# GpSimd drains, separate value banks and a split slot end in a chunked attention and mixture-of-experts kernel

## Chip, cores and metric

The kernel runs on one core of a Trainium2 chip. The metric is the device time of one execution in microseconds. The core's engines are TensorE (PE, matrix products; its weight loads are shown apart as PEld), VectorE (DVE), ScalarE (ACT), GpSimd (POOL) and SyncE (SP). Each engine works through an instruction queue of its own, and engines wait for each other and for transfers on semaphores. Sums of matrix products lie in PSUM banks of 128 x 512 floats.

## Reference

Attention within chunks of 64 positions, then a top-1 mixture of experts over the 4608 rows that come out. q, k and v are 8 x 8 x 576 x 64, the gate is 512 x 8, w1 is 8 x 512 x 1024 and w2 is 8 x 1024 x 512, all float32.

```python
# attention, chunk = 64
scores = scale * np.matmul(q_c, k_c.transpose(0, 1, 2, 4, 3))
scores = scores - np.max(scores, axis=-1, keepdims=True)
attn = np.exp(scores)
attn = attn / (np.sum(attn, axis=-1, keepdims=True) + 1e-09)
out = np.matmul(attn, v_c)
# mixture of experts on x = out as [4608, 512]
logits = x @ w_gate
expert_idx = np.argmax(logits, axis=1)
gate_w = softmax(logits)[row, expert_idx]
for e in range(E):
    h = np.maximum(x[mask] @ w1[e], 0.0)
    out[mask] = gate_w[mask, None] * (h @ w2[e])
```

## The kernel before

**Attention.** A loop of 18 steps (`for g in range(NG)`) takes 256 rows each. A step computes scores into bank pair psS, a softmax on DVE and ACT, transposes, and then `attn_v`: 32 small products of weights and values into the two-bank tile psX (`pair["X"]`), one bank for each half of the heads. `x_out` (L292 to L301) scales each bank on DVE by the softmax sums. Routing follows two steps behind, and GpSimd stores the rows sorted by expert into a scratch tensor `xd` with indirect transfers (L426).

**Experts.** The rows are then worked through in slots of 256 sorted rows. Slot 0 is filled into the end of the attention. The others are `slot(u, ...)` (L1061), of which 17 are executed here. A slot whose expert has a small rest takes 64 or 128 more rows (`form_x`), all others take `form_a`; which one is decided at run time by a branch. For each of 8 parts f of the hidden layer, `gemm1` makes 12 products into bank psS or psL. ACT takes the rectified value `hh`, DVE the remainder `hl`, and two parts later `gemm2` adds 3 products for each half m of the rows into banks U and V, which are the two halves of psX. All operands are split into a high and a low part, so each product is three.

**The end of a slot.** After the branch come, in the order in which they are written (the order on PE, DVE, ACT and POOL is that of the code): `make_xt(u + 1)` transposes the rows of the next slot on PE, ACT and DVE split them; `split_step(u, 7)` splits one weight chunk (ACT L74, DVE L75) and issues an indirect weight load on GpSimd (L530); blocks 6 and 7 of `gemm2`; then `finish` for m = 0 and 1: DVE scales the sums by the gate into y (L670), and GpSimd writes y to its rows of the output with an indirect transfer (L671).

**GpSimd's queue in a slot** holds, from there on: the weight load, two output transfers, three gathers of rows (L545, the third after the branch), three weight loads (L530), and, where a `form_a` branch has to count up a semaphore for the transfer that only `form_x` makes, an instruction that the profile calls INC_SWDGE_SEM (L1128). All 205 indirect transfers of an execution are issued by GpSimd. At the end of the program (L1153 for the slots that are not executed, L1185 for the end itself) GpSimd waits for its transfers, executes such an INC_SWDGE_SEM and a DRAIN, and then all engines meet.

Of the kernel before, what the change touches and what calls it, by code (L numbers as in the profile page):

```python
# [8 lines left out]
F32 = mybir.dt.float32  # L9
# [3 lines left out]
AF = mybir.ActivationFunctionType  # L13
ALU = mybir.AluOpType
# [4 lines left out]
P = 128  # L19
# [5 lines left out]
G = 2  # L25
# [20 lines left out]
def attn_moe_kernel(ctx: ExitStack, tc: tile.TileContext, q, k, v, wg, w, out):  # L46
    nc = tc.nc
# [29 lines left out]
    def split_half(c, m, buf):  # L77
# [6 lines left out]


    psa = ctx.enter_context(tc.tile_pool(name="psa", bufs=1, space=PSUM))
    pair = {"X": psa.tile([P, 2, 512], F32, name="psX")}
    one = {x: psa.tile([P, 512], F32, name=f"ps{x}") for x in "TQLK"}
    c2 = ExitStack()
    pss = c2.enter_context(tc.tile_pool(name="pss", bufs=1, space=PSUM))  # L90
    pair["S"] = pss.tile([P, 2, 512], F32, name="psS")

    slots = {"U": [pair["X"][:, 0, :]], "V": [pair["X"][:, 1, :]], "X": [one["L"]],
             "TQ": [one["T"], one["Q"]], **{x: [one[x]] for x in "TQLK"}}
    turns = {x: 0 for x in slots}
    psum = []

    def bank(tag, shape):
        n = 1
        for x in shape[1:]:  # L100
            n *= x
        if tag == "S":
            t = psum[0].tile([P, 512], F32, name="psS", tag="S", bufs=2)
        else:
            t = slots[tag][turns[tag] % len(slots[tag])]
            turns[tag] += 1
        t = t[0:shape[0], 0:n]
        if len(shape) == 3:
            t = t.rearrange("p (a b) -> p a b", b=shape[2])
        return t  # L110
# [5 lines left out]
    gate = [const.tile([P, 3], F32, name=f"gate{i}") for i in range(3)]  # L116
    oid = [const.tile([P, 3], I32, name=f"oid{i}") for i in range(3)]

    NK, NB = 3, 3
# [9 lines left out]
    vb = [kv.tile([P, G, 512], F32, name=f"vb{i}") for i in range(NB)]  # L129
# [83 lines left out]
    def quads(i, hp):  # L213
        for c in range(2):
            for m in range(2):
                o = hp * 128 + c * 64
                yield (slice(c * 64, (c + 1) * 64), m, slice((i * 4 + hp) * 64, (i * 4 + hp + 1) * 64),
                       slice(m * 64, (m + 1) * 64), slice(o, o + 64), (m * 64, c * 64))
# [5 lines left out]
                             ones.unsqueeze(1).broadcast_to([P, 4, P]), start=True, stop=True)  # L224

    def scores(g):
        ps = pair["S"]
        for i in range(G):
            for hp in range(4):
                for po, m, fo, pi, fi, at_ in quads(i, hp):  # L230
                    nc.tensor.matmul(ps[po, m, fo], qt[g][pi, i, fi], kb[g % NK][pi, i, fi],
                                     start=True, stop=True, tile_position=at_)
        return ps
# [37 lines left out]
    def attn_t(ex):  # L271
        at = sp.tile([P, G, 4, 128], F32, name="at", bufs=1)
        for i in range(G):
            pt = bank("TQ", [P, 4, 128])
            for hp in range(4):
                nc.tensor.transpose(pt[:, hp, :], ex[:, i * 4 + hp, :, :].rearrange("p m k -> p (m k)"), ident)
            nc.scalar.copy(at[:, i, :, :], pt)
        return at

    def attn_v(g, at):  # L280
        px = pair["X"]
        for i in range(G):
            for hp in range(4):
                for po, m, fo, pi, fi, at_ in quads(i, hp):
                    nc.tensor.matmul(px[po, m, fo], at[pi, i, hp, po], vb[g % NB][pi, i, fi],
                                     start=True, stop=True, tile_position=at_)
        return px

# [2 lines left out]
    def x_out(g, px, ri, xt):  # L291
        r0 = g * G % RB  # L292

        t = g * G - XB * RB
        assert t < 0 or t in stored
        for m in range(2):
            nc.vector.tensor_tensor(
                xt[:, r0:r0 + G, m * 256:(m + 1) * 256].rearrange("p i (h d) -> p i h d", d=64),
                px[:, m, :].rearrange("p (i h d) -> p i h d", i=G, d=64),
                ri[:, m * NH // 2:(m + 1) * NH // 2, :].rearrange("p (i h) o -> p i h o", i=G)  # L300
                .broadcast_to([P, G, 4, 64]), ALU.mult)  # L301

# [222 lines left out]
    def wset(u):  # L525

        return 0 if u < 2 else (u + 1) % 2
# [22 lines left out]
    def gather(u):  # L550
        for h in range(2):
            rows_in(xg[u % 2][h], u, h)
# [4 lines left out]
    def ids(u, t, h):  # L557

        nc.vector.tensor_copy(gate[u % 3][:, h:h + 1], t[:, D:D + 1])
        nc.vector.scalar_tensor_tensor(oid[u % 3][:, h:h + 1], past(u, h), BIG, t[:, D + 1:D + 2],  # L560
                                       ALU.mult, ALU.max)

    def make_xt(u, part=None, banks="TQ"):
        par = u % 2
        for h in range(2) if part is None else (part,):
            pg = bank(banks[h], [P, 4, 128])
            for kc in range(4):
                nc.tensor.transpose(pg[:, kc, :], xg[par][h][:, kc * 128:(kc + 1) * 128], ident)
            o = xhi[:, :, h * 128:(h + 1) * 128]
            nc.scalar.copy(o, pg)  # L570
            nc.vector.tensor_tensor(xlo[:, :, h * 128:(h + 1) * 128], pg, o.bitcast(F32), ALU.subtract)  # L571
            ids(u, xg[par][h], h)
# [92 lines left out]
        nc.tensor.matmul(py, hh, wl, start=False, stop=False)  # L665
        nc.tensor.matmul(py, hl, wh, start=False, stop=f == 7)  # L666

    def finish(u, m, py, n=P):
        y = yp.tile([P, D], F32, name=f"y{m}")[0:n, :]
        nc.vector.tensor_scalar(y, py, gate[u % 3][0:n, m:m + 1], None, ALU.mult)  # L670
        nc.gpsimd.indirect_dma_start(  # L671
            out=outs[m], out_offset=bass.IndirectOffsetOnAxis(ap=oid[u % 3][0:n, m:m + 1], axis=0),
            in_=y, in_offset=None,
            bounds_check=NT - 1, oob_is_err=False)
# [258 lines left out]
    for g in range(NG):  # L933
        ga, gl = g - 1, g - 2
        pace[0] = 1000
        ps = scores(g)
# [6 lines left out]
        if ga >= 0:  # L943
            at = attn_t(st_e[ga])
# [17 lines left out]
        if ga >= 0:  # L962
            px = attn_v(ga, at)
# [14 lines left out]
    g = NG - 1  # L978
# [5 lines left out]
    at = attn_t(ex)  # L984
# [11 lines left out]
    px = attn_v(g, at)  # L996
# [64 lines left out]
    def slot(u, kd, nxt):  # L1061
        par = wset(u)
        py = [bank("UV"[m], [P, D]) for m in range(2)]
        if u > 1:
            gather(u + 2)

        last = [[hq.tile([P, BLK], F32R, name=f"{x}{f}") for x in ("hh", "hl")] for f in (6, 7)]

        def block(f, h, ms=(0, 1)):
            for m in ms:  # L1070
                gemm2(par, f, h, m, py)

        def later():

            if u == 1:
                yield from places()
            yield from find_u(u + 3)

        def some(x, n):
            for _ in range(n):  # L1080
                next(x, None)

        def form_a():
            h = []
            x = later()
            for f in range(8):
                h.append(gemm1(par, f, *(last[f - 6] if f > 5 else ())))
                if f == 4 and u + 1 < SMAX:

                    tc.mark_branch_hint_location(f"kind{u + 1}", hint=(nxt + 1) >> 1, engines=PE)  # L1090
                if f == 0 and u > 1:
                    gather_x(u + 1)
                if f < 7:
                    split_step(u, f)
                    some(x, 4 if u == 1 else 1)
                if f > 1:
                    block(f - 2, h[f - 2])

        def form_x(n):

            make_xt_x(u, n)
            pe = bank("K", [n, D])
            h = []
            x = later()

            def more(f):
                gemm2_pe(par, f, *h[f][1], pe)

            for f in range(8):
                h.append(gemm1_x(par, f, n, *(last[f - 6] if f > 5 else ())))  # L1110
                if f == 4 and u + 1 < SMAX:
                    tc.mark_branch_hint_location(f"kind{u + 1}", hint=(nxt + 1) >> 1, engines=PE)
                if f == 0 and u > 1:
                    gather_x(u + 1)
                if f < 7:
                    split_step(u, f)
                    some(x, 4 if u == 1 else 1)
                if 1 < f < 7:
                    block(f - 2, h[f - 2][0])
                    more(f - 2)  # L1120
            more(5)
            more(6)
            block(5, h[5][0], (0,))
            more(7)
            finish(u, 2, pe, n)
            block(5, h[5][0], (1,))

        with tc.If(kd > 0, label=f"kind{u}") as c:  # L1128
            with tc.If(kd < 2) as c2:
                form_x(EXT // 2)  # L1130
            with c2.Else():
                form_x(EXT)
        with c.Else():
            form_a()
        make_xt(u + 1)
        split_step(u, 7)
        for f in (6, 7):
            block(f, last[f - 6])
        for m in range(2):
            finish(u, m, py[m])  # L1140

    n_s = nc.values_load(kind[0:1, NU:NU + 1], min_val=0, max_val=SMAX)
    PE = [mybir.EngineType.PE]
# [45 lines left out]
```

## Time and profile before

| | us |
|---|---|
| median of 3 runs (lowest, highest) | 646.58 (644.78, 647.96) |
| the profiled execution's own time | 638.72 |
| its span, first to last instruction | 636.7 |
| attention, up to about | 162 |
| one plain slot, from one slot's y to the next one's | 23.4 |
| PE busy | 584.4 (92%) |
| DVE / ACT / POOL busy | 421.0 / 288.7 / 273.1 |

The profile lists every instruction of one execution with start and duration. Names ending in q (POOLq, SPq) are an engine's sequencer: branches, semaphore instructions and drains. They are not counted as busy. "Idle before" is an engine's idle time ahead of an instruction, with what ended it.

### The profile page before, as it was taken

The numbers are of one execution on the slowest core, as the hardware profiler recorded it, in microseconds if no ns is written. First come the engines' busy times: TensorE is split into PE (matmuls) and PEld (weight loads), VectorE is DVE, ScalarE is ACT, GpSimd is POOL, SyncE is SP. The second block draws the span as 40 slices with busy tenths as digits, with TensorE's granted clock in tenths as the row PEclk, the third lists the DMA queues.
The fourth block names the chain that finished last, engine by engine and source line by source line (L and its number), as shares of the span: only waits on it lengthen the run. The fifth ranks groups of instructions, "written<-read, shape, count | busy, mean of one in ns | idle before, by whom it ended". The sixth has DMA issues, their size and how long they took to land. (4 is left out here: it accounts for less than half of the span.)

```text
span 636.7 us, 14562 instructions
## 1 busy us (share of the span) xinstructions
PE 584.4 (92%) x5775; PEld 513.1 (81%) x5775; DVE 421.0 (66%) x831; ACT 288.7 (45%) x544; POOL 273.1 (43%) x277
## 2 busy tenths in 40 slices
PE   8796979899799999999999999998999999999980
PEld 5575767678698999988788799897989989999970
DVE  6687988977365776774666376674647767766750
ACT  1575656662133554543444255452434545545440
POOL 2123544475522743741435163463116437436430
PEclk8998999999899999999999999998999999999995
DMA  8979888433654611362146020557302146111100
GB/s 312 394 269 351 304 314 295 169 155 123 228 213 148 206 49 39 126 214 79 42 168 216 5 79 29 174 187 258 116 18 77 39 164 213 48 33 35 35 5 31
DMA packets 31901, 94.87 MB, mean 149 GB/s; under 512 B 11488, under 2 KB 11488, under 8 KB 28192
## 3 DMA queue, kind: packets, MB, share of 16 engines
q0 software_dynamic: 20880, 60.74, 27.7%
q1 hardware_dynamic: 10896, 32.53, 14.2%
q8 instruction: 71, 1.16, 0.8%
q14 instruction: 54, 0.44, 0.2%
HBM read 122.65 MB, written 19.96 MB: 224 GB/s over the span
## 5 line engine op out<-in xcount | busy, mean ns | idle before, releaser
L75 DVE TENSOR_TENSOR wlo<-raw,whi 128x1024 fp32r<-128x1024 f32 x134 | 163.7, 1222 | 38.0 <-ACT whi L74 37.9
L530 POOL DMA_INDIRECT raw<-in_w,widx x71 | 74.5, 1049 | 195.3 <-DVE wlo L75 156.7
L74 ACT CAST whi<-raw 128x1024 fp32r<-128x1024 f32 x134 | 140.2, 1046 | 0.4 <-DMA raw<-in_w,widx 0.4
L608 ACT ACTIVATE hh<-psS 128x256 fp32r<-128x256 f32 x110 | 42.4, 385 | 180.9 <-PE psS L588 88.5
L664 PE MATMUL psX<-whi,hh 128*128 128x512 f32 x288 | 115.2, 400 | 0.0
L665 PE MATMUL psX<-wlo,hh 128*128 128x512 f32 x288 | 113.4, 394 | 0.0
L666 PE MATMUL psX<-whi,hl 128*128 128x512 f32 x288 | 112.5, 391 | 0.0
L588 PE MATMUL psS<-xhi,whi 128*128 128x256 f32 x344 | 97.4, 283 | 0.2 <-DVE oid L560 0.2
L588 PE MATMUL psS<-xlo,whi 128*128 128x256 f32 x344 | 97.4, 283 | 0.3 <-DVE xlo L571 0.3
L588 PE MATMUL psS<-xhi,wlo 128*128 128x256 f32 x344 | 97.3, 283 | 0.0
L613 DVE SCALAR_TENSOR_TENSOR hl<-psS,hh 128x256 fp32r<-128x256 f32 x110 | 46.4, 422 | 74.5 <-ACT hh L608 37.4
L545 POOL DMA_INDIRECT xg<-xd,idx x58 | 80.5, 1388 | 22.7 <-issue 15.2
L671 POOL DMA_INDIRECT out_y<-y,oid x40 | 53.6, 1339 | 42.1 <-DVE y L670 36.3
L588 PEld LDWEIGHTS psS<-xhi,whi 128*128 128x128 f32 x344 | 65.7, 191 | 4.0 <-ACT xhi L570 0.5
L588 PEld LDWEIGHTS psS<-xlo,whi 128*128 128x128 f32 x344 | 65.7, 191 | 3.2 <-DVE xlo L571 0.5
L588 PEld LDWEIGHTS psS<-xhi,wlo 128*128 128x128 f32 x344 | 65.7, 191 | 0.0
L666 PEld LDWEIGHTS psX<-whi,hl 128*128 128x128 f32 x288 | 54.1, 188 | 12.2
L664 PEld LDWEIGHTS psX<-whi,hh 128*128 128x128 f32 x288 | 54.5, 189 | 8.1 <-issue 0.4
L665 PEld LDWEIGHTS psX<-wlo,hh 128*128 128x128 f32 x288 | 54.5, 189 | 6.9
L82 POOL TENSOR_TENSOR wlo<-raw,whi 128x512 fp32r<-128x512 f32 x16 | 20.4, 1273 | 66.6 <-ACT whi L81 52.1
L426 POOL DMA_INDIRECT xd<-xb,di x32 | 31.8, 993 | 16.6 <-issue 5.6
L571 DVE TENSOR_TENSOR xlo<-psT,xhi 128x512 fp32r<-128x512 f32 x17 | 11.8, 692 | 27.5 <-ACT xhi L570 27.5
(220 smaller groups left out, 1013.5 us busy)
## 6 DMA issues: line engine op xcount, KB each, us to landing
vb<-in_v SPq DMA_DIRECT2D x18, 512.0 KB, 6.2
kb<-in_k SPq DMA_DIRECT2D x17, 512.0 KB, 6.6
qt<-in_q SPq DMA_DIRECT2D x17, 512.0 KB, 7.5
raw<-in_w SPq DMA_DIRECT2D x16, 256.0 KB, 7.0
raw<-in_w,widx POOLq DMA_INDIRECT x71, 2.6
xg<-xd,idx POOLq DMA_INDIRECT x58, 3.9
out_y<-y,oid POOLq DMA_INDIRECT x40, 4.0
kb<-in_k SPq DMA_DIRECT2D x2, 256.0 KB, 3.7
```

Source lines behind the costliest of these rows:

```text
L74: nc.scalar.copy(hi, src)
L75: nc.vector.tensor_tensor(lo, src, hi.bitcast(F32), ALU.subtract)
L426: nc.gpsimd.indirect_dma_start(out=xds[b % 2 * NMAX + i], out_offset=bass.IndirectOffsetOnAxis(ap=di[:, i, :], axis=0), in_=x, in_offset=N ...
L530: nc.gpsimd.indirect_dma_start(out=raw[c][:, :], out_offset=None, in_=w, in_offset=bass.IndirectOffsetOnAxis(ap=widx[:, u, c:c + 1], axis= ...
L545: nc.gpsimd.indirect_dma_start(out=t[:, :], out_offset=None, in_=xd[0:rows, :], in_offset=bass.IndirectOffsetOnAxis(ap=place(u, h), axis=0 ...
L588: nc.tensor.matmul(ph, a, b[:, kc, 0:BLK], start=kc + i == 0, stop=kc + i == 5)
L608: nc.scalar.activation(hh, ph, AF.Relu)
L613: nc.vector.scalar_tensor_tensor(hl, ph, 0.0, hh.bitcast(F32), ALU.max, ALU.subtract)
L664: nc.tensor.matmul(py, hh, wh, start=f == 0, stop=False)
L665: nc.tensor.matmul(py, hh, wl, start=False, stop=False)
L666: nc.tensor.matmul(py, hl, wh, start=False, stop=f == 7)
L671: nc.gpsimd.indirect_dma_start(out=outs[m], out_offset=bass.IndirectOffsetOnAxis(ap=oid[u % 3][0:n, m:m + 1], axis=0), in_=y, in_offset=No ...
```

## The change

1. `nc.gpsimd.drain()` is written once in each slot, behind the branch and ahead of `make_xt(u + 1)`. It has no semaphore of its own, neither a wait nor an update. It stands in POOL's queue behind the third weight load (or, after `form_x`, behind that branch's output transfer) and ahead of the weight load of `split_step(u, 7)`.
2. Banks U and V become two tiles of their own, where they were the halves of one tile of two banks. `attn_v` and `x_out` address them as `px[m]`. The banks stay the same ones.
3. The last two blocks of a slot are computed for m = 0 first, then for m = 1, and each half is finished at once. The first half is scaled by ACT, the second by DVE as before. `finish` in slot 0 and for `form_x`'s extra rows stays on DVE.

```diff
-    pair = {"X": psa.tile([P, 2, 512], F32, name="psX")}
-    one = {x: psa.tile([P, 512], F32, name=f"ps{x}") for x in "TQLK"}
+    one = {x: psa.tile([P, 512], F32, name=f"ps{x}") for x in "UVTQLK"}
...
-                    nc.tensor.matmul(px[po, m, fo], at[pi, i, hp, po], vb[g % NB][pi, i, fi],
+                    nc.tensor.matmul(px[m][po, fo], at[pi, i, hp, po], vb[g % NB][pi, i, fi],
...
-                px[:, m, :].rearrange("p (i h d) -> p i h d", i=G, d=64),
+                px[m].rearrange("p (i h d) -> p i h d", i=G, d=64),
...
-    def finish(u, m, py, n=P):
+    def finish(u, m, py, n=P, on_act=False):
         y = yp.tile([P, D], F32, name=f"y{m}")[0:n, :]
-        nc.vector.tensor_scalar(y, py, gate[u % 3][0:n, m:m + 1], None, ALU.mult)
+        if on_act:
+            nc.scalar.activation(y, py, AF.Copy, scale=gate[u % 3][0:n, m:m + 1])
+        else:
+            nc.vector.tensor_scalar(y, py, gate[u % 3][0:n, m:m + 1], None, ALU.mult)
...
+        nc.gpsimd.drain()
         make_xt(u + 1)
         split_step(u, 7)
-        for f in (6, 7):
-            block(f, last[f - 6])
         for m in range(2):
-            finish(u, m, py[m])
+            for f in (6, 7):
+                block(f, last[f - 6], (m,))
+            finish(u, m, py[m], on_act=m == 0)
```

PE's last 12 products of a slot, before. The names hh_3988 and hl_3989 are part 6, hh_3990 and hl_3991 part 7; the first three rows of a part are m = 0, the next three m = 1.

```order
L664 MATMUL psX<-whi_7_2976,hh_3988 128x512
L665 MATMUL psX<-wlo_7_2984,hh_3988 128x512
L666 MATMUL psX<-whi_7_2976,hl_3989 128x512
L664 MATMUL psX<-whi_7_2976,hh_3988 128x512
L665 MATMUL psX<-wlo_7_2984,hh_3988 128x512
L666 MATMUL psX<-whi_7_2976,hl_3989 128x512
L664 MATMUL psX<-whi_7_2976,hh_3990 128x512
L665 MATMUL psX<-wlo_7_2984,hh_3990 128x512
L666 MATMUL psX<-whi_7_2976,hl_3991 128x512
L664 MATMUL psX<-whi_7_2976,hh_3990 128x512
```

The first 10 of the same 12 products after the change:

```order
L662 MATMUL psU<-whi_7_2977,hh_3990 128x512
L663 MATMUL psU<-wlo_7_2985,hh_3990 128x512
L664 MATMUL psU<-whi_7_2977,hl_3991 128x512
L662 MATMUL psU<-whi_7_2977,hh_3992 128x512
L663 MATMUL psU<-wlo_7_2985,hh_3992 128x512
L664 MATMUL psU<-whi_7_2977,hl_3993 128x512
L662 MATMUL psV<-whi_7_2977,hh_3990 128x512
L663 MATMUL psV<-wlo_7_2985,hh_3990 128x512
L664 MATMUL psV<-whi_7_2977,hl_3991 128x512
L662 MATMUL psV<-whi_7_2977,hh_3992 128x512
```

U is complete after 6 of the 12 products, where it was complete after 9; V stays last. The number of products is the same.

POOL around the end of the same slot, before, with the semaphores each waits for (ISA is the INC_SWDGE_SEM of the branch):

```order
L530 DMA raw_67<-in_w,widx 128x2048 [waits DMASW7_49,DVE_49]
L1128 ISA [waits DMASW0_49]
L1128 UNCONDITIONAL_BRANCH
L530 DMA raw_2967<-in_w,widx 128x2048 [waits DMASW1_49,DVE_49]
L671 DMA out_y<-y_4768,oid_109 4608x512 [waits DMASW2_49,DMASW0_49,DVE_49]
L671 DMA out_y<-y_4773,oid_109 4608x512 [waits DMASW3_49,DVE_49]
L1151 TENSOR_LOAD kind
```

And after:

```order
L528 DMA raw_67<-in_w,widx 128x2048 [waits DMASW7_49,DVE_49]
L1129 ISA [waits DMASW0_49]
L1129 UNCONDITIONAL_BRANCH
L528 DMA raw_2968<-in_w,widx 128x2048 [waits DMASW1_49,DVE_49]
L672 DMA out_y<-y_4765,oid_110 4608x512 [waits DMASW2_49,DMASW0_49,Activation_49]
L672 DMA out_y<-y_4776,oid_110 4608x512 [waits DMASW3_49,DVE_49]
L1154 TENSOR_LOAD kind
```

The order of the transfers is the same, and the first output transfer waits for ACT where it waited for DVE. Drains are not listed in this view: the added one stands behind the branch, ahead of the load into raw_2968.

## Rows read from the trace of the kernel before

**Rows 1.** The page: busy us by engine (share of the span) and instructions.
```profile
PE 584.4 (92%) x5775; PEld 513.1 (81%) x5775; DVE 421.0 (66%) x831; ACT 288.7 (45%) x544; POOL 273.1 (43%) x277
```
**Rows 2.** Stretches: length, then PE, PEld, DVE, ACT, POOL busy; clock, DMA share, GB/s.
```profile
0.00:162.00 162.00, 138.05 (x3070) 112.19 (x3071) 127.01 (x283) 85.44 (x204) 68.58 (x112) 0.96 0.74 268
...
480.00:620.00 140.00, 138.59 (x896) 125.72 (x894) 97.75 (x168) 69.66 (x108) 70.97 (x54) 1.00 0.23 74
620.00:637.00 17.00, 0.00 (x0) 0.00 (x0) 0.05 (x1) 0.00 (x0) 2.04 (x2) 0.58 0.08 29
```
**Rows 3.** Timeline, last GpSimd work: start, us, engine, line, operation [idle before].
```profile
619.00 0.99 POOL L530 DMA_INDIRECT raw<-in_w,widx  x1 [7.19 <-DVE wlo L75]
620.30 1.03 POOL L671 DMA_INDIRECT out_y<-y,oid  x1 [0.30 <-DVE y L670]
621.64 1.00 POOL L671 DMA_INDIRECT out_y<-y,oid  x1 [0.31 <-DVEq L1153]
```
**Rows 4.** Queue instructions of L1153 and L1185: ns min/median/max, first and last start.
```profile
L1153 POOLq EVENT_SEMAPHORE  x5: 17/43/2316, 622.7 to 623.1; - x5
...
L1153 POOLq INC_SWDGE_SEM  x1: 2148/2148/2148, 625.4 to 625.4; - x1
...
L1185 POOLq EVENT_SEMAPHORE  x4: 17/17/17, 635.9 to 636.6; - x4
L1185 POOLq DRAIN  x3: 46/107/8062, 627.8 to 636.4; - x3
L1185 SPq DRAIN  x3: 7/7/13, 628.3 to 636.1; - x3
```
**Rows 5.** GpSimd's drain at the program's start, and ACT's drains at its end.
```profile
L1179 POOLq DRAIN  x1: 187/187/187, 0.3 to 0.3; - x1
...
L1185 ACTq DRAIN  x2: 8/8/8, 618.8 to 636.1; - x2
```
**Rows 6.** The largest group of GpSimd's transfers, from the page.
```profile
L530 POOL DMA_INDIRECT raw<-in_w,widx x71 | 74.5, 1049 | 195.3 <-DVE wlo L75 156.7
```
**Rows 7.** GpSimd's timeline: behind form_x at 207 and 368, and in plain slots.
```profile
207.27 1.02 POOL L530 DMA_INDIRECT raw<-in_w,widx  x1 [2.64 <-DVE wlo L75]
...
368.89 1.01 POOL L530 DMA_INDIRECT raw<-in_w,widx  x1 [4.05 <-DVE wlo L75]
...
407.56 0.99 POOL L530 DMA_INDIRECT raw<-in_w,widx  x1 [2.22 <-DVE wlo L75]
415.75 0.99 POOL L530 DMA_INDIRECT raw<-in_w,widx  x1 [7.20 <-DVE wlo L75]
```
**Rows 8.** INC_SWDGE_SEM at 326.5 and at 383.9 us, columns as in Rows 4.
```profile
L1128 POOLq INC_SWDGE_SEM  x1: 2170/2170/2170, 326.5 to 326.5; - x1
...
L1128 POOLq INC_SWDGE_SEM  x1: 414/414/414, 383.9 to 383.9; - x1
```
**Rows 9.** Timeline of PE, ACT and DVE at a plain slot's end.
```profile
386.93 0.38 ACT L608 ACTIVATE hh<-psS 128x256 fp32r<-128x256 f32 x1 [1.50 <-PE psS L588]
...
387.35 0.42 DVE L613 SCALAR_TENSOR_TENSOR hl<-psS,hh 128x256 fp32r<-128x256 f32 x1 [0.66 <-ACT hh L608]
...
388.91 0.48 PE L664 MATMUL psX<-whi,hh 128*128 128x512 f32 x1
...
389.72 1.06 ACT L74 CAST whi<-raw 128x1024 fp32r<-128x1024 f32 x1
...
390.15 0.39 PE L666 MATMUL psX<-whi,hl 128*128 128x512 f32 x1
...
391.97 1.41 DVE L670 TENSOR_SCALAR y<-psX,gate 128x512 f32<-128x512 f32 x2
...
393.51 0.39 ACT L608 ACTIVATE hh<-psS 128x256 fp32r<-128x256 f32 x1 [2.73 <-DVE y L670]
```
**Rows 10.** Groups: an ACT copy of 512 columns from PSUM, and attention's x_out.
```profile
L277 ACT COPY at<-psT 128x512 f32<-128x512 f32 x18 | 10.6, 587 | 19.6 <-PE psT L276 19.6
...
L297 DVE TENSOR_TENSOR xb<-psX,ri 128x512 f32<-128x512 f32 x32 | 20.6, 686 | 4.0 <-PE psX L285 2.9
```

More of the change, by code (lines that the diff above doesn't have):

```diff
@@ L86, in attn_moe_kernel @@
     psa = ctx.enter_context(tc.tile_pool(name="psa", bufs=1, space=PSUM))
-    pair = {"X": psa.tile([P, 2, 512], F32, name="psX")}
-    one = {x: psa.tile([P, 512], F32, name=f"ps{x}") for x in "TQLK"}
+    one = {x: psa.tile([P, 512], F32, name=f"ps{x}") for x in "UVTQLK"}
     c2 = ExitStack()
     pss = c2.enter_context(tc.tile_pool(name="pss", bufs=1, space=PSUM))
-    pair["S"] = pss.tile([P, 2, 512], F32, name="psS")
-    slots = {"U": [pair["X"][:, 0, :]], "V": [pair["X"][:, 1, :]], "X": [one["L"]],
-             "TQ": [one["T"], one["Q"]], **{x: [one[x]] for x in "TQLK"}}
+    pair = pss.tile([P, 2, 512], F32, name="psS")
+    slots = {"X": [one["L"]], "TQ": [one["T"], one["Q"]], **{x: [one[x]] for x in one}}
     turns = {x: 0 for x in slots}
@@ L226, in scores @@
     def scores(g):
-        ps = pair["S"]
+        ps = pair
         for i in range(G):
@@ L280, in attn_v @@
     def attn_v(g, at):
-        px = pair["X"]
+        px = [one["U"], one["V"]]
         for i in range(G):
```

## Prediction

> **What bounds the kernel now.** I read the page's busy times first: PE is busy for 92% of the span [rows 1]. The stretches sharpen that: in the attention it is busy for 138.05 of 162 us, and from 480 to 620 us, six plain slots, for 138.59 of 140 at a granted clock of 1.00 [rows 2]. So in the slots PE sets the pace, and an edit that moves neither the number of PE's products nor a wait of PE gains nothing there. The last stretch is another matter: from 620 to 637 us PE, ACT and DVE do practically nothing, and GpSimd is busy for 2.04 us only [rows 2]. 17 us belong to the end of the program, and busy times don't say what fills them. The queue instructions do [rows 3, 4]: the last output transfer is issued from 621.64 to 622.64; GpSimd waits 2.32 us for landings, up to 625.4; an INC_SWDGE_SEM runs for 2.15 us, up to 627.6; then a DRAIN runs for 8.06 us, from 627.8 to 635.8, and right behind it GpSimd's barrier instructions start at 635.9. SP had reached its own drains of the end at 628.3, and ACT at 618.8 [rows 4, 5]. For 7.5 us everybody waits for one GpSimd drain. That is what the change can reach.
>
> **The change part by part.**
>
> **1. The added drains.** What does a GpSimd drain cost, and what sets its cost? Four are in the trace. With no transfer issued since the start it took 0.19 us [rows 5]; with all 205 transfers behind it, 8.06; the two that follow it, with none in between, 0.107 and 0.046 [rows 4]. So it isn't a fixed price of the instruction: it is paid for something that has piled up, and a drain clears it. Neither is it a wait for data, since the landings were waited for by 625.4, ahead of it. The reading that asks for least is a price per transfer issued since the last drain: 8.06 / 205 = 0.039 us each (the largest group of them is 71 weight loads [rows 6]). This is an estimate from one row. By it, of the 17 added drains the first one finds about 55 transfers, 55 x 0.039 = 2.1 us, and each later one about 9, (205 - 55 - 3) / 16 x 0.039 = 0.36 us.
>
> Do these hide? The drain stands behind the third weight load and ahead of the weight load of the slot's last step, which waits for DVE's split of a chunk, in a plain slot with 7.20 us of idle time in front of it; after a form_x slot with 2.64 us (the first slot) or 4.05 us [rows 7]. 2.1 and 0.36 us fit into these gaps. What is queued behind the drain is that weight load, the two output transfers, three gathers and two more loads. If the cover were too short by x, they would all come x later; the queue has another pause of 2.22 us in the same slot, ahead of the load at 407.56 [rows 7], which takes up that much before PE could see any of it. So I cost the added drains at 0.
>
> The last drain then finds 3 transfers, the load and the two outputs of [rows 3]: 3 x 0.039 = 0.12, with a floor between 0.05 and 0.19 us [rows 4, 5]; say 0.2 us. It would end at 628.0. Then SP is last, with its drains at 628.3 to 628.4. The barriers behind it take as long as now, from 635.9 to the span's end at 636.7, 0.8 us. New end: 628.4 + 0.8 = 629.2. Saved: 636.7 - 629.2 = **7.5 us**. (Of the 8.06 us, 0.2 stay and about 0.4 go to SP.)
>
> The Trainium skill speaks against this: its page "VectorE: DVE Perf Modes", section "The DRAIN you can't avoid", says that the drains of a program's preamble and postamble are about 12 ns each, constant, on all five engines. By that the last drain is worth nothing and nothing can be saved. Here ACT's took 8 ns and SP's 7 to 13 [rows 4, 5], which agrees, but GpSimd's took 8062 ns; the measurement decides, and the rule holds here for the other engines only.
>
> **2. INC_SWDGE_SEM at the end.** It stands on the same chain, with 2.15 us [rows 4]. Its price also grows: 2.17 us at 326.5, 0.41 at 383.9, and 2.15 at 625.4 again [rows 4, 8]. It falls back without any drain, so something else than a drain sets it back. Whether a drain does so too no row shows. From below, a fall to the 0.41 saves 1.7 us more on the chain, since SP's end waits behind it as well; from above nothing changes. I take no change, because the one fall in the trace happened without a drain.
>
> **3. Halves, and ACT for the first.** PE's products are the same 12, only in another order; the part-7 operands are needed 3 products (0.7 us) earlier. hh and hl of part 7 were ready at 387.31 and 387.77, and the first of the 12 starts at 388.91 [rows 9], so there is no wait: 0. U is complete about 0.7 us earlier, with the product at 390.15 [rows 9]. ACT has its chunk split until 390.78, then the scaling, by the nearest row a copy of 512 columns from PSUM, 0.59 us [rows 10]; DVE's form takes 1.41 for two, 0.70 each [rows 9]. ACT is done by about 391.4, and its next work starts at 393.51 [rows 9]: it lies in idle time of 2.7 us. DVE loses 0.7 us in each of 17 slots, 12 us that nobody waits for. What stands behind the scaling on ACT is the branch and the next slot's first hh. And at the program's end? The output transfers are not held by y but by each other: load at 619.00, outputs at 620.30 and 621.64, with 0.30 us between each [rows 3]. y earlier by 0.7 us moves neither. The load waits for the chunk split, which stays. So 0; if the transfers did follow y, the gain would be at most 0.7 us, and if ACT's wait came late, the loss about 0.6 us.
>
> **4. Two tiles instead of one.** x_out's first half on DVE may start one small product earlier, and the second half has a wait of its own. DVE waited 2.9 us in all for these products [rows 10]; that bounds the gain, and 18 added waits at 17 ns, what a semaphore instruction takes in GpSimd's queue [rows 4], bound the loss at 0.3 us. PE's waits don't change, and PE is the busier of the two in the attention, 138.05 us to DVE's 127.01 [rows 2]. I take 0.
>
> **Sum.** The profiled execution took 638.72 us with a span of 636.7. 638.72 - 7.5 = 631.2 us for such an execution. The timed runs lie 7.9 us above it, with a median of 646.58, for a reason that no view shows; I take the saving over to them as it is: 646.58 - 7.5 = **639.1 us**.
>
> **The rivals.**
>
> *The second step falls too.* If a drain also sets back what INC_SWDGE_SEM pays for, the end is shorter by another 1.7 us: 637.4. For it: its growth of about 2 us [rows 8] looks like the same kind of piling up. Against: it was set back once with no drain. Chance 0.30.
>
> *The last drain stays.* Its 8.06 us may be a price that any drain pays once a single transfer has been issued since the drain before: the trace has drains after 205 transfers and after none, nothing in between. Then each added drain takes 8.06 us too. In a plain slot that is 0.9 over the 7.20 us, and the pause of 2.22 us takes it up. In the last slot the load at 619.00 and the outputs come 0.9 us later. Time: 646.58 + 0.9 = 647.5. The change then wouldn't do what it does on paper. Chance 0.17. The Trainium skill's rule named above, constant drains, would end at the same verdict, with no gain.
>
> *Slower.* As before, but the drain also waits for transfers under way, 8.06 us on top of a weight load's landing, taken as 2.3 us like the landing wait of [rows 4]: 10.4 us. From 7.20 + 2.22 = 9.4 us on, GpSimd's queue no longer catches up in a plain slot, and falls behind by 1.0 us in each. The six plain slots before the end, from 480 us on, add 6 us, and the last drain's own overhang 3.2: the last output transfer comes about 9 us later. Time: 655.6. Against it: 8.06 us started only when everything had landed. Chance 0.06.
>
> *In between.* The price goes partly with something that a drain doesn't clear, and about half of the 7.5 us is saved: 642.8. Chance 0.05.
>
> **How the numbers follow.** Forecast 0.42, the second step as well 0.30, stays 0.17, slower 0.06, in between 0.05. The runs scatter by about 1.5 us around their median, so the forecast's own range is 637.5 to 640.7 and that of the second rival begins at about 635.7. Up to 646.8 the range also takes in the case in between and a third of the runs in which the drain stays; what is left out is then under 0.2. 0.5% of the time is 3.2 us, about what a measurement here can tell from no change. Faster by more: 0.42 + 0.30 + most of the 0.05, 0.76. Within: 0.17. Slower: 0.07.
>
> **What the profile after would show.** Right: the last GpSimd DRAIN far under 1 us, 17 new ones, the first of about 2 us and the others under 0.5, and the span's end about 1 us behind SP's drains; PE's busy time within 1 us of 584.4, and the last PE product at about 618. If the last INC_SWDGE_SEM is near 0.4 us, the second step fell too. Wrong: a last drain of some 8 us, or drains of 8 us in the slots with the load behind them at a later start; ACT's scaling followed by a late hh, or PE pauses at a slot's start, would show the third part wrong.

## The result, and the profile after

| | before | after |
|---|---|---|
| median of the timed runs (lowest, highest), us | 645.68 (642.83, 647.96) | 637.32 (633.91, 641.31) |
| ratio, with its 95% interval | | 0.9874 (0.9826 to 0.9922) |
| the profiled execution's own time | 638.72 | 635.64 |
| its span | 636.7 | 633.8 |
| start of the last PE product | 618.20 | 625.04 |
| from there to the span's end ("the tail" below) | 18.5 | 8.7 |

The medians lie 8.4 us apart, and the interval of the ratio stands for 5.0 to 11.2 us. 9.8 us of the tail went. The two profiled executions show only 2.9 us of that in their spans, because PE reached its last product 6.8 us later in the one of after. That lateness has a place of its own in the attention, which is looked at behind the experiments: the last product ahead of the first y starts at 164.02 before and at 172.61 after, 8.6 us later. The plain slots take 23.42 us in both. One slot with `form_x` gives 1.8 us back: from last product to last product it takes 39.30 us before (438.36 to 477.66) and 37.47 after (447.03 to 484.50). In the profile before, PE's granted clock was 0.81 in that slot's first 9 us, where after has 1.00 (columns of [rows 2]):

```profile
438.36:447.40 9.04, 6.40 (x28) 5.80 (x27) 3.32 (x8) 2.03 (x4) 6.09 (x6) 0.81 0.63 212
```

Page of the profile after, busy us by engine, where [rows 1] stand for before:

```profile
PE 588.0 (93%) x5775; PEld 515.8 (81%) x5775; DVE 409.7 (65%) x814; ACT 298.6 (47%) x561; POOL 271.1 (43%) x277
```

17 instructions went from DVE to ACT, DVE's busy time fell by 11.3 us and ACT's rose by 9.9; PE's products are as many as before, but its busy time is 3.6 us longer.

The end of the program, which answers to [rows 3, 4]. First the timeline (start, us, engine, line, operation, idle before), then the queue instructions of the two lines at the end (count, ns min/median/max, first and last start):

```profile
625.04 0.39 PE L664 MATMUL psV<-whi,hl 128*128 128x512 f32 x1
...
625.85 0.99 POOL L528 DMA_INDIRECT raw<-in_w,widx  x1 [7.20 <-DVE wlo L75]
627.15 1.03 POOL L672 DMA_INDIRECT out_y<-y,oid  x1 [0.30 <-issue]
628.49 1.00 POOL L672 DMA_INDIRECT out_y<-y,oid  x1 [0.31 <-DVEq L1156]
```

```profile
L1156 POOLq EVENT_SEMAPHORE  x5: 17/43/1425, 629.8 to 630.2; - x5
...
L1156 POOLq INC_SWDGE_SEM  x1: 242/242/242, 631.6 to 631.6; - x1
...
L1188 POOLq EVENT_SEMAPHORE  x4: 17/17/17, 633.0 to 633.7; - x4
L1188 POOLq DRAIN  x3: 46/111/356, 632.6 to 633.5; - x3
L1188 SPq DRAIN  x3: 7/7/13, 632.6 to 633.2; - x3
```

The long DRAIN is gone: 0.36 us where it was 8.06. INC_SWDGE_SEM fell too, from 2.15 to 0.24. Step by step from the last product's start, before and after: to the landing of the last output 7.2 and 6.6; INC_SWDGE_SEM 2.15 and 0.24; from its end to the start of the drain 0.2 and 0.7, with a branch in between; the drain 8.06 and 0.36; what follows it 0.85 and 0.84. The differences are -0.6, -1.9, +0.5, -7.7 and 0, together -9.8 before rounding. The landing's 0.6 is no sure gain: it takes from 6.6 to 7.1 us in the profiles of the experiments below that keep this order of drain and transfers, and no run tells why.

The 17 new drains stand in line L1137. All of them, then the first, the longest and the last:

```profile
L1137 POOLq DRAIN  x17: 2365/4202/8267, 211.8 to 617.8; - x17
...
L1137 POOLq DRAIN  x1: 5659/5659/5659, 211.8 to 211.8; - x1
...
L1137 POOLq DRAIN  x1: 8267/8267/8267, 439.8 to 439.8; - x1
...
L1137 POOLq DRAIN  x1: 2379/2379/2379, 617.8 to 617.8; - x1
```

They are far longer than forecast, 2.4 to 8.3 us. What they cost is read from the load behind them. This is GpSimd's timeline around the longest one:

```profile
439.66 0.99 POOL L528 DMA_INDIRECT raw<-in_w,widx  x1 [2.22 <-DVE wlo L75]
...
448.94 0.99 POOL L528 DMA_INDIRECT raw<-in_w,widx  x1 [8.29 <-DVE y L671]
```

The load came after a pause of 8.29 us, where the usual pause at this place is 7.20: about 1 us late. In the other plain slots the pause is 7.20 as in [rows 7], or 6.30 in the first of them, so the drain lies inside a wait that was there anyway. Behind `form_x` it doesn't always: in the first slot the load came after 5.44 us, where [rows 7] have 2.64, and the next slot still took 23.42 us.

The end of a plain slot, where [rows 9] stand for before (timeline):

```profile
398.83 0.40 PE L664 MATMUL psU<-whi,hl 128*128 128x512 f32 x1
...
399.35 0.70 ACT L669 ACTIVATE y<-psU,gate 128x512 f32<-128x512 f32 x1
...
400.20 0.39 PE L664 MATMUL psV<-whi,hl 128*128 128x512 f32 x1
400.42 0.28 PE L586 MATMUL psS<-xhi,whi 128*128 128x256 f32 x1
...
400.65 0.75 DVE L671 TENSOR_SCALAR y<-psV,gate 128x512 f32<-128x512 f32 x1
...
402.19 0.38 ACT L606 ACTIVATE hh<-psS 128x256 fp32r<-128x256 f32 x1 [2.15 <-PE psS L586]
```

ACT scales the first half while PE computes the second, and then still waits for 2.15 us. The next slot's first product starts 0.22 us behind the last one of this slot: PE doesn't pause.

### The profile page after: what moved, and what is told of

Read it like the earlier page. It is cut to its first block, busy times and chain, and to the rows that moved or that the text cites. A ratio compares the mean times of both kernels' runs of the same rounds, so it can differ in the third digit from the quotient of the medians.

```text
span 633.8 us, 14583 instructions
## 1 busy us (share of the span) xinstructions
PE 588.0 (93%) x5775; PEld 515.8 (81%) x5775; DVE 409.7 (65%) x814; ACT 298.6 (47%) x561; POOL 271.1 (43%) x277
## 5 line engine op out<-in xcount | busy, mean ns | idle before, releaser
L662 PE MATMUL psU<-whi,hh 128*128 128x512 f32 x144 | 58.5, 406 | 0.0
L663 PE MATMUL psU<-wlo,hh 128*128 128x512 f32 x144 | 57.0, 396 | 0.0
L662 PE MATMUL psV<-whi,hh 128*128 128x512 f32 x144 | 56.7, 394 | 0.0
L663 PE MATMUL psV<-wlo,hh 128*128 128x512 f32 x144 | 56.4, 392 | 0.0
L664 PE MATMUL psU<-whi,hl 128*128 128x512 f32 x144 | 56.3, 391 | 0.0
L664 PE MATMUL psV<-whi,hl 128*128 128x512 f32 x144 | 56.2, 390 | 0.0
L662 PEld LDWEIGHTS psV<-whi,hh 128*128 128x128 f32 x144 | 27.0, 188 | 6.6
```

The lines of the kernel that those rows point to most:

```text
L662: nc.tensor.matmul(py, hh, wh, start=f == 0, stop=False)
```

## The experiments

The tail is compared, rather than the time, where a step of it is in question, since it is nearly the same in every profile of one kernel (8.7 us in three profiles of after, 6.5 and 6.7 in two of the kernel with the moved load) while the last product's start scatters by 15 us from profile to profile. The first four kernels below shared their runs of before (median 637.43 us), the next four theirs (647.18), and the last two theirs (647.86). The first four ran on another chip than the other six.

### The drains alone

```diff
+        nc.gpsimd.drain()
         make_xt(u + 1)
         split_step(u, 7)
```

The kernel before with this one line more.

> The kernel before with the one drain per slot added and nothing else of the change. Theory A (the drains are the whole gain: they take the last GpSimd drain from 8.06 to about 0.36 us and the last INC_SWDGE_SEM from 2.15 to about 0.24): from the last PE product's start to the span's end about 8.7 us, as in the changed kernel, against 18.5 before; ratio about 0.985. Theory B (the halves and ACT's scaling carry a part): the ratio is nearer to 1 than that, 0.99 or more, with a tail of over 9.5 us.

Median 626.75 us, ratio 0.9837 (0.9750 to 0.9923).

```profile
L1154 POOLq INC_SWDGE_SEM  x1: 242/242/242, 619.4 to 619.4; - x1
...
L1186 POOLq DRAIN  x3: 46/111/357, 620.3 to 621.2; - x3
```

Both steps fall as in the profile after, within a nanosecond. The tail is 8.7 us. One line makes the whole difference in the tail.

### Everything but the drains

```diff
-        nc.gpsimd.drain()
         make_xt(u + 1)
```

The changed kernel without that line: two tiles, halves, and ACT for the first half.

> The changed kernel without the drains: two tiles, halves, ACT's scaling alone. Theory A: the last drain is 8.06 us again, the last INC_SWDGE_SEM 2.15, the tail 18.5 us, ratio 1.00 within 0.005; the two output transfers at the end still stand 0.3 us apart behind the weight load, 3.4 us after the start of the last product. Theory B: a gain of 0.7 to 2 us, with the output transfers issued earlier after the last product.

Median 635.29 us, ratio 0.9969 (0.9928 to 1.0009): no difference that can be told. Queue instructions at the end, and the last output transfer:

```profile
L1155 POOLq INC_SWDGE_SEM  x1: 2148/2148/2148, 621.5 to 621.5; - x1
...
L1187 POOLq DRAIN  x3: 46/107/8062, 623.8 to 632.4; - x3
```

```profile
617.87 1.00 POOL L672 DMA_INDIRECT out_y<-y,oid  x1 [0.31 <-DVEq L1155]
```

The tail is 18.3 us. INC_SWDGE_SEM and the drain have the durations of [rows 4] again, and the last output transfer starts 3.44 us behind the start of the last product (614.43), as in before (621.64 - 618.20) and in after (628.49 - 625.04, 3.45). An earlier y doesn't move it: the queue of transfers holds it.

### The changed kernel once more

> The changed kernel once more, unchanged. In its first profile PE paused for about 5 us around 137 to 143 us ('issue') and then ran 5 us at half clock, so that the last product came 6.8 us later than before. If that is a property of the change (another number of instructions on PE's queue), it stands at the same place again. If it is a matter of the single execution, it is missing here or stands elsewhere, and the last product is near 618 us. The tail is 8.7 us either way.

Median 626.26 us, ratio 0.9805 (0.9725 to 0.9885), tail 8.7 us, of which the line is

```profile
L1188 POOLq DRAIN  x3: 46/111/356, 625.7 to 626.6; - x3
```

Beside `drain_only`, on the same chip, the two times differ by 0.5 us.

### One drain only, in slot 2, 5 or 8

```diff
+        if u == 2:      # 5, 8
+            nc.gpsimd.drain()
         make_xt(u + 1)
```

The kernel before with a single drain. In the order of the queue, 64, 92 or 120 transfers stand ahead of it, which leaves 141, 113 or 85 between it and the end; the expectations for slots 2 and 5 are off by one there. This tells what the last drain pays for.

> The kernel before with one drain only, in slot 2, after 63 of the 205 transfers. If the drain's price goes by transfers issued since the last drain (0.24 us + 0.038 each, fitted to 8.06 for 205 and 0.36 for 3), the last drain has 142 transfers and takes 5.6 us. If it is a price that any drain pays, 8.06. If it goes by the place that INC_SWDGE_SEM's price shows, far less. INC_SWDGE_SEM: if a drain sets it back to the start, it falls to about 0.4 in the next slot, grows by 0.18 a slot up to about 109 transfers later, falls again by itself, and is about 0.9 at the end; if not, 2.15 at the end.

> The kernel before with one drain, in slot 5, after 91 of the 205 transfers: 114 remain for the last one. Theory P (the price goes by the place that INC_SWDGE_SEM shows: about 0.08 us for each transfer since a drain or since the place fell back by itself, which it does some 110 transfers on): the place has just fallen back, INC_SWDGE_SEM is 0.3 to 0.5 us at the end and the last drain 0.4 to 1.6 us. Theory N (by the number of transfers since the last drain, at the 0.022 us that the slot-2 run's 3.07 for 142 gives): 2.5 us. Theory F (fixed): 8.06.

> The same with the drain in slot 8, after 120 transfers: only 85 remain. Theory P: no fall-back since, INC_SWDGE_SEM 1.9 us at the end and a last drain of 6.5 to 7 us, that is more than with 114 remaining. Theory N: 1.9 us. Theory F: 8.06.

Single times: 631.8, 644.16 and 643.15 us. Queue instructions at the end, slot 2, then 5, then 8:

```profile
L1155 POOLq INC_SWDGE_SEM  x1: 922/922/922, 624.7 to 624.7; - x1
...
L1187 POOLq DRAIN  x3: 46/107/3072, 625.8 to 629.5; - x3
```

```profile
L1155 POOLq INC_SWDGE_SEM  x1: 2448/2448/2448, 629.3 to 629.3; - x1
...
L1187 POOLq DRAIN  x3: 46/107/9284, 632.0 to 641.8; - x3
```

```profile
L1155 POOLq INC_SWDGE_SEM  x1: 1888/1888/1888, 631.2 to 631.2; - x1
...
L1187 POOLq DRAIN  x3: 46/107/6997, 633.3 to 640.8; - x3
```

A fixed 8.06 us is excluded: the same last drain takes 3.07, 9.28 or 7.00. So is a price by the number of transfers since the drain before alone, since with 141 of them it takes the least. Up to 113 transfers the price is a straight line: with 3 (after), 85 and 113 transfers it is 0.356, 6.997 and 9.284, which is (6.997 - 0.356) / 82 = 0.081 us per transfer and then (9.284 - 6.997) / 28 = 0.082, on top of some 0.12.

With the drain in slot 2 the price had grown and fallen back once by itself on the way, which INC_SWDGE_SEM shows at 110 and at 119 transfers since the drain:

```profile
L1128 POOLq INC_SWDGE_SEM  x1: 2377/2377/2377, 539.8 to 539.8; - x1
...
L1128 POOLq INC_SWDGE_SEM  x1: 481/481/481, 563.2 to 563.2; - x1
```

In slot 5's kernel it had not fallen back at 113 (2.45). My expectation for slot 5 put the fall ahead of that and missed. The two prices go together: the last drain is 0.36 + 4.04 x (the last INC_SWDGE_SEM - 0.242), a line laid through after and before, which gives 3.11, 9.27 and 7.01 for these three. Whatever both walk through, a drain empties it, and without one it falls back by itself, here somewhat above 110 transfers. It does not fall to the start: INC_SWDGE_SEM is 0.242 with 3 transfers and 1.888 with 85, so 0.020 each, and by that the 0.481 answer to about 15 transfers, where at most 9 or 10 had been issued since the fall. In before, by the drain's price, the 8.06 us answer to about 98 transfers ((8.06 - 0.12) / 0.081), 107 fewer than the 205. What it is that falls back stays open.

The single drains themselves fit this, with 64, 92 and 120 transfers ahead of them: 5.29, 8.61 and 2.46 us, where 0.12 + 0.081 each gives 5.3 and 7.6, and the third comes behind a fall-back. The second is 1.0 us above the price; the next experiment has a reason for that.

### The drain at the slot's very end

```diff
-        nc.gpsimd.drain()
         make_xt(u + 1)
         split_step(u, 7)
         for m in range(2):
             for f in (6, 7):
                 block(f, last[f - 6], (m,))
             finish(u, m, py[m], on_act=m == 0)
+        nc.gpsimd.drain()
```

Here the two output transfers are under way when the drain starts, and the gathers are queued behind it.

> The changed kernel with the drain moved behind the slot's two output transfers, where three gathers and two loads are queued right behind it. Theory W (a drain waits until what is under way has landed, and GpSimd's pauses take that up): each drain lasts 3 us or more from the second output's issue, the gathers start some 3 us later, the pause of 2.2 us ahead of the third load is gone and the third load at most 1 to 2 us late; PE's products keep their pace (13 plain slots of 23.4 us) and the tail is 8.7 us within 0.5. Theory S (a drain with transfers queued behind it holds up PE): plain slots get longer than 23.6 us, and the ratio loses 0.5% or more against the changed kernel.

Median 644.18 us, ratio 0.9961 (0.9925 to 0.9998): most of the gain is lost.

```profile
L1143 POOLq DRAIN  x17: 4952/6047/9830, 214.2 to 628.5; - x17
...
L1156 POOLq EVENT_SEMAPHORE  x5: 17/43/43, 636.0 to 636.4; - x5
...
L1156 POOLq INC_SWDGE_SEM  x1: 183/183/183, 636.5 to 636.5; - x1
...
L1188 POOLq DRAIN  x3: 40/111/119, 638.4 to 639.1; - x3
```

```profile
407.10 1.05 POOL L543 DMA_INDIRECT xg<-xd,idx  x1 [3.42 <-issue]
...
630.12 1.00 POOL L672 DMA_INDIRECT out_y<-y,oid  x1 [0.31 <-DVEq L1156]
```

With the outputs under way none of the 17 drains takes less than 4.95 us, so a drain does wait for them. The plain slots keep their pace of 23.4 us all the same, although the gathers come 3.42 us later: the queue's pauses take that up. In one slot they don't. Behind the longest drain (9.83 us) the first gather comes 8.51 us behind the last output transfer, and PE pauses for 3.8 us ahead of the transposes of a `form_x` branch, where the three profiles of after have 1.4 to 1.7 (GpSimd's timeline, then PE's waits from 438 to 488 us):

```profile
458.02 1.05 POOL L543 DMA_INDIRECT xg<-xd,idx  x1 [8.51 <-issue]
```

```profile
PE psT L575 <- issue: 3.8, 1, 3.8
```

That slot takes 41.1 us, 3.6 more than in the profile after. Theory S, a drain that holds up PE, was right there, and theory W in the plain slots. The tail is 12.7 us, 4.0 more than in after, and here I had expected 8.7. The two together are 7.6 us, and the median is 7.4 us above that of the changed kernel in `after_pair`, on the same chip. The drain is over at 633.49 and GpSimd's next instruction in the list comes at 636.0, 2.5 us later, with the slot's closing branch in between; from INC_SWDGE_SEM to the last drain it is another 1.8 us where it was 0.7. In after the same branch runs ahead, at 626.91, while the output transfers are still being worked off, and the next instruction comes at 629.82; since the last output is issued until 629.49, little of that shows. A drain right ahead of the branch lays it bare.

### No load ahead of the last outputs

```diff
                 if f == 0 and u > 1:
                     gather_x(u + 1)
+                    load_w(u + 1, 2)
...
         nc.gpsimd.drain()
         make_xt(u + 1)
-        split_step(u, 7)
+        split_chunk(wset(u + 1), 5)
```

The changed kernel with a slot's last weight load issued in the next slot. It aims at the tail that is left: the load ahead of the two outputs.

> The changed kernel with the slot's last weight load moved behind the next slot's third gather, so that nothing stands between the drain and the two output transfers. Theory A (at the end the outputs were held by that load, not by y): the first output is issued right after ACT's scaling, about 0.1 us before the start of the last product, the second about 1.45 us after that start instead of 3.44, and the tail falls from 8.7 to about 6.7 us; ratio about 0.003 below the changed kernel's. Rival: the load, now issued at the slot's start, comes late for the chunk that ACT splits in part 6, plain slots get longer than 23.4 us, and the gain is lost.

Median 633.88 us, ratio 0.9831 (0.9783 to 0.9880). Timeline of GpSimd's end, and the queue instructions:

```profile
624.98 1.31 POOL L672 DMA_INDIRECT out_y<-y,oid  x1 [6.51 <-ACT y L669]
626.60 1.00 POOL L672 DMA_INDIRECT out_y<-y,oid  x1 [0.30 <-issue]
```

```profile
L1190 POOLq DRAIN  x3: 46/107/210, 630.0 to 631.1; - x3
L1190 SPq DRAIN  x3: 7/7/13, 630.5 to 630.8; - x3
```

Only here does the first half's earlier y count: the first output transfer waits for ACT's y and starts 0.1 us behind the last product, where it was 2.1. The load ahead of it is gone: this kernel issues 204 transfers, since the load in question was for a slot that doesn't run. The tail is 6.5 us. What is left of it does not end with the landing: behind the branch of 626.10 GpSimd's next instruction comes at 629.07, 1.5 us after the last output was issued, and none of its waits there takes longer than 43 ns. To see whether the shorter tail arrives in the time, this kernel and the changed one ran side by side:

> The changed kernel, unchanged, once more, to stand beside best_pair on one chip. Its ratio to the kernel before: 0.980 to 0.988 as in the earlier two comparisons; its stretch from the start of the last PE product to the span's end 8.7 us, give or take 0.2, whatever the time of the last product is.

> The changed kernel with the last weight load of a slot issued in the next slot, so that no load stands ahead of the two last output transfers. Theory E (what is saved in the stretch behind the last product is saved in the time): the stretch is 6.5 us again, 2.2 less than in after_pair, and the median of the timed runs lies 2.2 us, give or take 1.5, under that of after_pair. Theory G (the moved load costs PE something in the slots, which the tail gives back): the same 6.5 us behind the last product, but the median within 1 us of after_pair's or above it, with the last product's start later by some 2 us.

The changed kernel had 636.79 us (633.78 to 643.30), ratio 0.9826 (0.9776 to 0.9876); the one with the moved load 636.22 (632.24 to 643.55), ratio 0.9797 (0.9750 to 0.9845). The tails are 8.7 and 6.7. The medians differ by 0.57 us, where theory E asked for 0.7 to 3.7 and theory G for less than 1; the ratios differ by 0.0029, which would be 1.9 us. With runs that scatter over 10 us this tells neither apart. What the tail gives is shown; that it arrives in the time isn't. In both profiles with the moved load, the slot with `form_x` at about 450 to 487 us is longer by 0.9 to 1.2 us (38.46 and 38.36 where the changed kernel's three profiles have 37.24 to 37.47), but not for the same reason: once PE's granted clock was 0.79 to 0.85 for the first 9 us of it, once the pause ahead of the branch's transposes was 2.55 us where the changed kernel has 1.64. Whether the moved load does that stays open; the clock was as low at this place in before (39.30 us), without it. It beats the kernel before; that it beats the changed one isn't settled.

### Where the last product's lateness comes from

PE reached its last product between 612.8 and 628.0 us in the profiles. In the two kernels most alike, after and `again` (the same code), the difference is 6.9 us. Waits of PE from 130 to 150 us in after (line, waited for: us in total, times, longest), then two stretches of both with the columns of [rows 2]:

```profile
PE psU L283 <- issue: 2.5, 4, 1.1
PE psV L283 <- issue: 1.2, 3, 0.5
```

```profile
136.00:144.00 8.00, 4.28 (x72) 3.18 (x71) 1.51 (x8) 1.73 (x8) 4.71 (x5) 0.89 0.44 169
144.00:149.00 5.00, 5.00 (x31) 3.86 (x30) 2.31 (x7) 1.01 (x4) 0.74 (x1) 0.50 0.01 3
```

The same for `again`:

```profile
136.00:144.00 8.00, 8.00 (x129) 7.12 (x128) 5.65 (x23) 3.93 (x16) 5.96 (x8) 1.00 0.43 165
144.00:149.00 5.00, 5.00 (x44) 4.14 (x43) 2.25 (x12) 1.91 (x7) 3.44 (x6) 1.00 0.44 172
```

In after PE stops several times in `attn_v` with nothing that the profile names as the cause, and from 144 to 149 us its granted clock is 0.50, 1.2 GHz where `again` has 2.4. Is it the new tiles? One of the kernels with the old tile shows it too, the one with the drain in slot 8 (waits of PE, 130 to 150 us):

```profile
PE psX L285 <- issue: 3.5, 7, 1.0
```

So does slot 5's kernel. The pause was in the profiles of all kernels of the second and third group, whose runs of before lie at 647 to 648 us, and in none of the first group, at 637, where `no_drain` and `again` have the new tiles. So the new tiles are neither needed for it nor enough. Whether it goes with the session or with the chip isn't told apart. The profile of before, of the first measurement, shows no such pause. That would fit the gap that the prediction could not explain, 646.58 us timed against 638.72 profiled, but no profile of one of the slower executions of before was kept, so this isn't shown. What makes PE pause there is open.

## Why the prediction was right, and which of its steps were not

**The bound.** That everybody waits for one GpSimd drain was right, and shown by taking the drains away and by adding them alone. The term of the sum held: 7.5 us forecast, 7.7 measured for the drain. The time, 637.32, is 1.8 us under the 639.1 and just outside the forecast's own 637.5 to 640.7; the case that came true is the rival with 637.4. That the median comes so close to it is luck: the runs of after lie between 633.91 and 641.31, 3.4 and 4.0 us from their median where the prediction allowed for 1.5, and in the three later comparisons against shared runs of before the drains at this place were worth 10.7 to 11.2 us. The tail itself lost 9.8 us where the sum had 7.5.

**The added drains.** "Paid for something that has piled up, and a drain clears it" held. The price did not: 8.06 / 205 divides by all transfers, but the pile falls back by itself, and its 8.06 us answer to about 98 of them. The price is 0.081 us, twice the 0.039. At the end this made no odds, as 3 transfers cost little by either (0.2 us forecast, 0.36 measured). In the first slot it did: 2.1 us forecast, 5.66 measured.

**"Neither is it a wait for data"** was the step that failed. It was read from one drain, ahead of which everything had landed. In the slots, transfers are under way, and the drain waits for them too. The rival "slower" rested on this mechanism, with a landing of 2.3 us on top of 8.06. The size was wrong: with some 9 transfers since the drain before, the price is about 0.85 us, so most of the 2.4 us or more is wait. Where the pile is large the whole exceeds its price by 0 to 2.0 us: by 0 and 1.0 in the single drains of 5.29 and 8.61, by 1.1 in after's first (5.66, where 55 x 0.081 + 0.12 = 4.6) and by 2.0 in the first one with the moved load (6.61). In after's first, GpSimd's last packet lands 2.7 us behind the drain's start, which with the price would make 7.3 us. So the two overlap in part rather than add. The stretches of the longest drain in after, 439.80 to 448.06, show what it waited for (columns as in [rows 2]):

```profile
439.80:446.00 6.20, 6.20 (x39) 5.42 (x38) 3.17 (x7) 3.25 (x6) 0.85 (x1) 1.00 0.84 328
446.00:447.30 1.30, 1.30 (x7) 0.84 (x5) 1.30 (x4) 0.89 (x2) 0.00 (x0) 1.00 0.20 76
447.30:448.06 0.76, 0.12 (x1) 0.00 (x0) 0.76 (x2) 0.00 (x0) 0.00 (x0) 1.00 0.00 0
```

The transfers are busy for 0.84 of the first 6.2 us, and the drain ends 0.8 us after the last of them. Its cost to PE was still nothing in the plain slots, for the reason that the prediction gave: the pause of 7.20 us covers it, and where a drain was too long, the next pause took it up. PE's pace in the plain slots is 23.42 us (last products at 484.50 and 507.92 in after) as before. That this isn't so wherever a drain stands, the drain at the slot's very end shows.

**INC_SWDGE_SEM.** The forecast kept it at 2.15, and the rival "the second step falls too" (0.30) came true. Its argument against it, one fall without a drain, had not excluded a second cause: it falls both by itself and by a drain. 1.9 us, of which 0.5 went to the gap behind it: it has a branch in it, grew from 0.2 to 0.7 us and was on no row. Why it grew isn't shown; with the moved load, where INC_SWDGE_SEM is as short, it is 0.2.

**Who is last.** "Then SP is last" was wrong by little: GpSimd's drain ends at 632.9 and SP's start at 632.6. In the kernel with the moved load SP is last, as forecast.

**Halves, ACT and two tiles at 0.** Right as far as the runs tell: 0.9969 without the drains, an interval that holds 1 and leaves room for a gain of up to 4.6 us, a tail of 18.3 us where it was 18.5, and no pause of PE at the slot's end. The reason given, that the outputs are held by each other and by the load ahead, is what `best` then showed by taking the load away.

**The signs named.** Of what the profile after would show, the last drain, the 17 new ones and the last INC_SWDGE_SEM (0.24) came as said. The lengths of the new drains did not. Nor did PE's busy time within 1 us of 584.4 (588.0) and the last product at about 618 (625.04), and for both the stretch in the attention is the place that the profiles show: the same code in `again` has 585.0 and 618.16.

**A page.** The Trainium skill, "VectorE: DVE Perf Modes", section "The DRAIN you can't avoid", has drains at program ends as constant, about 12 ns. SP's agree here, 7 to 13 ns; GpSimd's last one took from 0.12 to 9.28 us in these kernels, so for it the measurement decides.

## What to carry to other kernels

Look behind the last product: a program that issues hundreds of indirect transfers from GpSimd can end in a drain that costs microseconds, and one drain placed inside a pause that GpSimd has anyway takes that price off the end. Put it ahead of a wait that is there already, with few transfers under way, and neither right ahead of a branch nor ahead of gathers that PE will soon want. One row tells that a price grows, but not by what: two more points, with the suspected quantity changed, are wanted before it is divided.

## What the runs showed of the hardware

- GpSimd's last drain took about 0.12 us and 0.081 more for each indirect transfer since the drain before: 0.119 with none (`drain_end`), 0.210 with 2 (moved load), 0.356 with 3, 6.997 with 85 and 9.284 with 113. INC_SWDGE_SEM grew along with it, by 0.020 for each (0.183, 0.224, 0.242, 1.888, 2.448). Both start over after a drain. Without one both fall back by themselves, between 110 and 119 transfers since the drain in the one place where that was narrowed down, and not quite to the start.
- In a slot a drain also waited for transfers under way, and took 2.4 to 9.8 us.
- Behind a drain, GpSimd's branch at the program's end took 2.5 us to its next instruction; in after the same branch lies beside the last output transfers.
- In the attention PE paused for 3.5 to 3.7 us in all without a named cause, in the profile after and in all profiles of the second and third group; in after its granted clock was 0.50, 1.2 GHz, for 5 us behind that.
